# The second batch's first k^T v in place of five unread matmuls, and the first transfers in another order

## The chip, the cores and the metric

The kernel runs on one core of one Trainium2 chip. The metric is device microseconds (us) of one execution; the kernel before took 843.87 us (median of 3 runs, 843.82 to 843.91).

## The reference

Two layers are computed one after the other, all in fp32.

```python
# attention without a softmax; batch 8, heads 8, sequence 576, head size 64
kv  = np.einsum('bhsd,bhse->bhde', k, v)
out = np.einsum('bhsd,bhde->bhse', q, kv)
rms = np.sqrt(np.mean(out * out, axis=-1, keepdims=True) + 1e-06)
x   = out / rms * g_norm                     # heads side by side: x is (8, 576, 512)
# mixing along the sequence by rank 32, then a feed-forward net of 512 -> 2048 -> 512
u   = x + (x.transpose(0, 2, 1) @ U @ V).transpose(0, 2, 1)
y   = u + np.maximum(u @ w_ch1, 0.0) @ w_ch2
```

`U` is 576x32 and `V` is 32x576. The two weights `w_ch1` and `w_ch2` reach the kernel as raw bits of 64-bit numbers and are decoded on the chip.

## The kernel before, in words

**Tiling.** The eight heads of a batch are four pairs (p = 0 to 3), 128 columns each. The 8 x 576 = 4608 tokens are nine blocks of 512. The feed-forward net works block by block with 16 slices of 128 of the 2048 hidden columns: `ffn1` computes a slice of the hidden layer into a PSUM tile `h` (for slice 0 of the first block into a tile `pp`), `relu` takes it to SBUF in two fp32r parts (`hhl`, high part by ScalarE, low part by VectorE), and `ffn2` multiplies it into four accumulators `y`. A product of two fp32 numbers is three fp32r products: high by high, high by low, low by high.

**Attention of a pair.** `kv_step` multiplies k^T v (PE) and copies it into `kvb` (ScalarE); `out_step` multiplies q by it (PE) and squares it (ScalarE, L358 and L359); `stats_step` sums the squares (VectorE, L369), takes a square root (ScalarE, L370) and three or four small VectorE steps (L371 to L374); `mul_step` scales the product into `x` (VectorE, L391 and L393). `turn_step` turns `x` by a product with the identity (PE, `wf`), `t_step` and `t4_step` form x U (PE, then ScalarE and VectorE L443), `mix_first` adds the product with V (PE) and splits the result into `uth` (ScalarE, L155) and `utl` (VectorE, L485), the operands of `ffn1`; `mix_rest` does the last 64 tokens. For batch 1 and later, one `kv_step` serves two pairs: 20 matmuls from the tile `kv_sb`.

**The first stage.** Before the feed-forward net can run, pairs 0 to 3 of batch 0 go through all of this one after the other. In the same time the first weights are decoded: ScalarE makes a cast (L130, `dec_104<-raw`, one shared buffer), VectorE combines it (L133), ScalarE casts the high part (L145, `ws` or L153, `w1s`), and VectorE subtracts the low part (L146 or L165). Each engine carries out its instructions in the order in which they stand in its program.

**What sets the order.** `PLAN` gives every step of the first stage a place (a number), the steps are issued in the order of these places, and then the scheduler of the language decides, from its own estimates of durations, how the instructions of an engine follow each other. From slice 13 of block 0 on (`pinned`), matmuls keep the order in which they are written. `LOADS` is the order in which the SyncE queue issues the first 19 transfers; after the first eight of them each waits for an earlier one to land. In `LOADS`, `kv0` is k and v of pair 0, `q0` its q, `w11` the `w_ch1` half of weight slice 1, `w21` its `w_ch2` half, `uv` is U and V, and `kv4` and `q4` are the k, v and q of batch 1's first pairs. `keep_warm` issues matmuls whose results nobody reads: `fill0=3` with pair 0 and `fill1=5` with pair 1, and `FILL` another nine.

Of the kernel before, what the change touches and what calls it, by code (L numbers as in the profile page):

```python
# [58 lines left out]
PREP = [37, 37, 41, 43, 47, 49, 53, 57, 56, 63, 63, 66, 66, 69, 75, 78]  # L59
RAWAT = [-1, -1, -1, -1, -1, -1, -1, -1, -1, -1, -1, -1]  # L60
CPAT = [8, 8, 10, 12, 12, 14, 16, 18, 18, 20, 22, 24, 26, 28, 30]
PLAN = dict(g=2, pair=(2, 7.5, 10.5, 13.5), kv=(-3, 0.5, 0, -1), out=(0, 2.5, 2, 2.5), stats=(2.5, 3, 2.5, 7.0), mul=(2.5, 5.5, 4.0, 8.5), tr=(11.5, 8.5, 10.5, 12.5), t=(14.0, 11.0, 12.5, 15.0), t4=(14.5, 16, 14, 17.0), mix=(25.5, 21.5, 27, 19.5), mt=(44.0, 41.0, 38.5, 46.5), uv=-6, v4=15, w0=33, x0=53, warm=12, fill0=3, fill1=5, fill2=0, fill3=0, d=(16.5, 17.5))
ENG = dict(u0='vgg', kv='aaaaa', xh='aaaaa', xl='vvvvv', t4='aaaa', te='aaaa', uh='aaaa', v4='ggga', wh='agg', wl='vvv', ab='vvv', u='va')
LOADS = ['kv0', 'uv', 'q1', 'q0', 'w10', 'kv1', 'w11', 'kv2', 'q2', 'q3', 'kv3', 'w13', 'w22', 'w23', 'w20', 'w12', 'w21', 'kv4', 'q4']
NBLK = B * S // BLK


# [1 line left out]
def build(ctx: ExitStack, tc: tile.TileContext, kv0_in, kv_in, q_in, uv_in, w_in, out):  # L69
# [19 lines left out]
    v4 = const.tile([P, S], F32R, name="v4")  # L89
# [11 lines left out]
    def mm(*args, **kw):  # L101
        ins = nc.tensor.matmul(*args, **kw)  # L102
        if pinned[0]:
            tc.keep_in_program_order(ins)
# [16 lines left out]
    def decode(raw, tmp, n=None, held=False):  # L121

        parts = raw.bitcast(BF16).rearrange("p (n t) -> p n t", t=4)
        size = parts.shape[1]
        top = tops[:, 0:size].bitcast(FP16).rearrange("p (n t) -> p n t", t=2)[:, :, 1]
        if n is None or ENG["ab"][n] == "a":
            nc.scalar.copy(out=top, in_=parts[:, :, 2])  # L130
        else:
            nc.vector.tensor_copy(out=top, in_=parts[:, :, 2])
        ins = nc.vector.scalar_tensor_tensor(out=tmp.bitcast(U32), in0=raw.bitcast(U32).rearrange("p (n t) -> p n t", t=2)[:, :, 0],  # L133
                                             scalar=13, in1=tops[:, 0:size].bitcast(U32), op0=ALU.logical_shift_right,
                                             op1=ALU.bitwise_or)
        if held:
            tc.keep_in_program_order(ins)
# [10 lines left out]
    def move(which, n, out, in_, mul=None):  # L148

        e = ENG[which][n]  # L150
        if e == "a":
            if mul is None:
                nc.scalar.copy(out=out, in_=in_)  # L153
            else:
                nc.scalar.mul(out=out, in_=in_, mul=mul)  # L155
        else:
            eng = nc.vector if e == "v" else nc.gpsimd
            if mul is None:
                eng.tensor_copy(out=out, in_=in_)
            else:  # L160
                eng.tensor_scalar(out=out, in0=in_, scalar1=mul, scalar2=None, op0=ALU.mult)

    def minus(which, n, out, in0, in1):
        eng = nc.vector if ENG[which][n] == "v" else nc.gpsimd
        eng.tensor_tensor(out=out, in0=in0, in1=in1, op=ALU.subtract)  # L165
# [39 lines left out]
    def load_w(f, w):  # L205
        if f not in raws:
            raws[f] = weight_slot(f"raw{f}", [P, 2, DM], I64, f)
        load_fields(raws[f][:, w], w_in[f][:, w], f >= 4)

    def keep(which, f, w):  # L210
        w_sb[which][f] = [[w[:, c // 2, s, (c % 2) * P:(c % 2 + 1) * P] for c in range(ND)] for s in range(2)]

    def halves(t):
        return t.rearrange("p (a c) -> p a c", a=2)

    def decode_first(which, tmp, n):
        decode(raws.pop(which), tmp, n)
        w = const.tile([P, 2, 2, DM // 2], F32R, name=f"{which}s0", tag=f"{which}_0")
        move("wh", n, w[:, :, 0], halves(tmp))
        minus("wl", n, w[:, :, 1], halves(tmp), w[:, :, 0].bitcast(F32))  # L220
        keep(which, 0, w)
        whole[which, 0] = w

    def decode_w(f, held=False):

        tmp = dec_tile(1)
        decode(raws.pop(f).rearrange("p w c -> p (w c)"), tmp, held=held)
        w = weight_slot(f"ws{f}", [P, 4, 2, DM // 2], F32R, f)
        t = tmp.rearrange("p (a c) -> p a c", a=4)
        split(w[:, :, 0], w[:, :, 1], t, nc.vector)  # L230
        for n, which in enumerate(("w1", "w2")):
            keep(which, f, w[:, 2 * n:2 * n + 2])
        whole[f] = w
# [69 lines left out]
    def bank():  # L303
        bank_no[0] += 1
        if startup[0] and bank_no[0] % (7 - NEARLY) >= 3 - NEARLY:
            return ps_y.tile([P, 512], F32, name="y")
        return ps_p.tile([P, 512], F32, name="pp")

    def kv_step(b, p):

        if b > 0 and p % 2:
            return
        m = loads.pop(("kv", b, p))
        pp = bank()
        if b == 0:
            kb = kvb[p % 2]
            for i in range(NT):
                for lo in (0, D):
                    own = slice(i * P + lo, i * P + lo + D)
                    mm(pp[lo:lo + D, 0:D], lhsT=m[:, own], rhs=m[:, NT * P:][:, own], start=(i == 0), stop=(i == NT - 1))  # L320
            for lo in (0, D):
                move("kv", p, kb[lo:lo + D, lo:lo + D], pp[lo:lo + D, 0:D])
            return
        tails = 4 * MAIN
        for a in range(2):
            for i in range(NT):
                k, v = (2 * a * MAIN + i * P, (2 * a + 1) * MAIN + i * P) if i < 4 else (tails, tails + (1 + a) * P)
                for lo in (0, D):
                    mm(pp[lo:lo + D, a * D:(a + 1) * D], lhsT=m[:, k + lo:k + lo + D], rhs=m[:, v + lo:v + lo + D],
                       start=(i == 0), stop=(i == NT - 1))  # L330
        for lo in (0, D):
            move("kv", -1, kvbs[lo:lo + D, :, lo:lo + D], pp[lo:lo + D, 0:2 * D].rearrange("p (a c) -> p a c", a=2))
# [44 lines left out]
    def plain(b, p):  # L377
        return b < len(T32) and T32[b][p] == "f"
# [290 lines left out]
    spare = ps_h.tile([P, BLK], F32, name="h")  # L669
    for _ in range(PLAN["warm"]):  # L670
        mm(spare[:, 0:P], lhsT=kvb[0], rhs=kvb[0], start=True, stop=True)
    nc.scalar.sqrt(out=root, in_=eps)
    x123 = weight_slot("x123", [P, NPAIR - 1, NT, P], F32, 15)
    x0 = [x_sb] + [x123[:, p] for p in range(NPAIR - 1)]
# [15 lines left out]
    uv = uvs[:, NUV:NUV + NUV // 2].bitcast(F32)  # L690
# [9 lines left out]
    for w, which in enumerate(("w1", "w2")):  # L700
        first[f"{which}0"] = lambda which=which: load_first(which)
        for f in range(1, 4):
            first[f"{which}{f}"] = lambda f=f, w=w: load_w(f, w)
    for name in LOADS:
        first[name]()
# [18 lines left out]

    tasks = [(PLAN["uv"], uv_step), (PLAN["v4"], v4_step), (PLAN["g"], g_step)]
    ahead = 1 + len(PLAN["d"])
    for f, place in enumerate(PLAN["d"]):
        tasks.append((place, lambda f=f: decode_w(1 + f, True)))
    for p in range(NPAIR):
        for name, what in (("kv", kv_step), ("out", out_step), ("stats", stats_step), ("mul", mul_step),  # L730
                           ("tr", turn_step), ("t", t_step), ("t4", t4_step)):
            tasks.append((PLAN["pair"][p] + PLAN[name][p], lambda what=what, p=p: what(0, p)))
        tasks.append((PLAN["pair"][p] + PLAN["mix"][p], lambda p=p: keep_warm(p, PLAN[f"fill{p}"])))
        tasks.append((PLAN["pair"][p] + PLAN["mix"][p], lambda p=p: mix_first(p)))
        tasks.append((PLAN["pair"][p] + PLAN["mt"][p], lambda p=p: mix_rest(p)))
    for place, n in FILL:
        tasks.append((place, lambda n=n: [mm(spare[:, 0:P], lhsT=kvb[0], rhs=kvb[0], start=True, stop=True) for _ in range(n)]))
    tasks.append((PLAN["w0"], lambda: decode_first("w1", early[0], 0)))
    tasks.append((PLAN["x0"], lambda: decode_first("w2", early[1], 2)))
    def next_load(load, b, p):  # L740
        nxt = (b, p + 1) if p + 1 < NPAIR else (b + 1, 0)
        if nxt[0] < B:
            load(*nxt)

    def split_step(b, p):
        if not plain(b, p):
# [3 lines left out]
                     t=t_step, t4=t4_step)  # L750
# [8 lines left out]
    tasks = {}  # L759
# [8 lines left out]
    def pair_tasks(b, p, base, steps):  # L768


        def run(*names):
            for name in names:
                attention[name](b, p)

        def o():
            run("out", "stats", "mul", *([] if plain(b, p) else ["turn"]))

        def t():
            run("t", "t4")

        for name, what in (("kv", lambda: run("kv")), ("kvl", lambda: next_load(load_kv, b, p + 1) if p % 2 == 0 else None), ("out", o),
                           ("ql", lambda: next_load(load_q, b, p)), ("split", lambda: run("split")), ("turn", lambda: run("turn") if plain(b, p) else None), ("t", t), ("mix", lambda: mix_step(b, p))):
            at(base + steps[name], what)

# [185 lines left out]
```

## Time and profile before

| | |
|---|---|
| median of 3 runs | 843.87 us |
| profiled execution: span from the first to the last instruction | 842.3 us |
| median less span | 1.6 us |
| TensorE busy | 831.6 us (99%) |
| VectorE busy | 605.4 us (72%) |
| ScalarE busy | 380.0 us (45%) |
| first `ffn2` matmul on TensorE (row `y<-hhl,w2s`) | 41.68 us after the start |

The profiled execution is one execution; its span leaves out what lies ahead of the first and behind the last instruction, and no other time of that execution is recorded. Matmuls overlap each other, so TensorE counts as busy for nearly the whole span; where it waits is read from the bracket at the end of a row of the timeline, `[0.75 <-ACT uth L155]`: 0.75 us idle before this row, ended by the ScalarE instruction that wrote `uth`. In a timeline row the first number is the start, the second the duration of the merged run of instructions, and `xN` their count; an fp32 matmul appears as two. The start of the next row less the start of this one is what the engine was taken up for. PE is TensorE, PEld its weight loads, ACT is ScalarE, DVE VectorE, POOL GpSimd and SPq the queue of SyncE.

### The profile page before, as it was taken

The page shows a single profiled execution, that of the slowest core. Times are in us where ns is not written, and L with a number is a line of the kernel's source. Part 1 is how long each engine was busy: PE and PEld are TensorE (multiplying, and loading weights), DVE is VectorE, ACT ScalarE, POOL GpSimd, SP SyncE. Part 2 cuts the span into 40 slices and gives each one's busy share as a digit, 9 for nine tenths or more (in the row PEclk, how much of TensorE's full clock was granted, in tenths as well). Part 3 has the DMA queues.
Part 4 walks back from the last instruction along what each step waited for, and adds up shares of the span by engine and source line. Part 5 has one row for each costly group of instructions (what it writes and reads, how often), then busy time and mean ns, then how long its engine had stood idle before and what let it go on. Part 6 is the DMA issues. An engine that isn't in the chain of part 4 may idle for free.

```text
span 842.3 us, 12663 instructions
## 1 busy us (share of the span) xinstructions
PE 831.6 (99%) x4581; PEld 694.3 (82%) x4581; DVE 605.4 (72%) x991; ACT 380.0 (45%) x663; POOL 8.3 (1%) x37
## 2 busy tenths in 40 slices
PE   8999999999999999999999999999999999999998
PEld 8888888888887888888888878888888888888886
DVE  4788655778898877767957898568667965762574
ACT  4766422333244444465436653644355444332431
POOL 3000000000000000000000000000000000000000
PEclk9999999999999999999999999999999999999999
DMA  9996975666487764577878678866765786666665
GB/s 339 385 375 227 370 261 213 237 202 196 139 288 255 222 182 139 162 239 240 258 226 285 208 227 253 273 212 193 228 206 174 224 268 204 184 187 211 193 202 175
DMA packets 105229, 195.00 MB, mean 232 GB/s; under 512 B 10320, under 2 KB 41296, under 8 KB 101456
## 3 DMA queue, kind: packets, MB, share of 16 engines
q1 hardware_dynamic: 105024, 194.07, 70.4%
q8 instruction: 37, 0.61, 0.3%
q14 instruction: 24, 0.20, 0.1%
q10 hardware_dynamic: 144, 0.13, 0.0%
HBM read 142.91 MB, written 51.25 MB: 231 GB/s over the span
## 4 chain that ended last, share of the span: by engine, by line
PE 89%; DVE 5%; DMA 4%; ACT 1%; issue 1%; SPq 0%; DVEq 0%; ACTq 0%
PE y L102 67%; PE h L102 13%; PE pp L102 9%; DMA w2s<-dec 1%; DMA kvq<-kv_in 1%; DMA w2s<-wf 1%; DMA w1s<-wf 1%; DVE dec L268 1%; DVE ss L369 1%; DVE hhl L525 1%; DVE dec L273 1%; ACT wf L145 1%; DMA ringw<-w2s 1%; DVE dec L146 0%; DVE dec L133 0%
## 5 line engine op out<-in xcount | busy, mean ns | idle before, releaser
L102 PE MATMUL y<-entry,ring 128*128 128x512 f32 x576 | 136.0, 390 | 0.0
L102 PE MATMUL y<-hhl,ws 128*128 128x512 f32 x540 | 132.3, 392 | 0.0
L102 PEld LDWEIGHTS y<-entry,ring 128*128 128x128 f32 x576 | 107.5, 188 | 22.2
L102 PE MATMUL h<-uth,ws 128*128 128x512 f32 x360 | 120.4, 395 | 1.4 <-ACT uth L155 0.7
L102 PEld LDWEIGHTS y<-hhl,ws 128*128 128x128 f32 x540 | 99.9, 188 | 20.1
L594 DVE TENSOR_TENSOR h<-y,h 128x512 f32<-128x512 f32 x71 | 48.6, 689 | 57.4 <-PE y L102 52.1
L102 PE MATMUL y<-uB,ringw 128*128 128x512 f32 x354 | 85.0, 391 | 0.0
L638 DVE TENSOR_TENSOR entry<-h,entry 128x1024 fp32r<-128x1024 f32 x48 | 58.6, 1220 | 35.0 <-ACT entry L637 34.8
L102 PE MATMUL y<-uT,ring 128*128 128x512 f32 x348 | 82.4, 390 | 0.0
L102 PEld LDWEIGHTS h<-uth,ws 128*128 128x128 f32 x360 | 67.5, 188 | 16.6 <-DVE hhl L525 1.7
L102 PEld LDWEIGHTS y<-uB,ringw 128*128 128x128 f32 x354 | 66.0, 188 | 13.6
L102 PEld LDWEIGHTS y<-uT,ring 128*128 128x128 f32 x348 | 65.0, 188 | 13.6 <-ACT h L601 0.2
L637 ACT CAST entry<-h 128x1024 fp32r<-128x1024 f32 x48 | 50.5, 1052 | 44.7 <-PE y L102 44.2
L102 PE MATMUL h<-utl,ws 128*128 128x512 f32 x180 | 70.3, 391 | 0.0
L524 ACT ACTIVATE hhl<-h 128x512 fp32r<-128x512 f32 x47 | 28.0, 596 | 76.4 <-PE h L102 76.3
L102 PE MATMUL y<-hhl,ringw 128*128 128x512 f32 x216 | 55.2, 390 | 0.5 <-DMA ringw<-w2s 0.5
L102 PE MATMUL y<-entry,ringw 128*128 128x512 f32 x216 | 55.1, 390 | 0.0
L102 PE MATMUL y<-uT,ringw 128*128 128x512 f32 x210 | 51.0, 391 | 0.0
L102 PEld LDWEIGHTS y<-hhl,ringw 128*128 128x128 f32 x216 | 40.4, 188 | 9.5 <-DMA ringw<-w2s 0.9
L102 PEld LDWEIGHTS y<-entry,ringw 128*128 128x128 f32 x216 | 40.3, 188 | 8.3
L525 DVE SCALAR_TENSOR_TENSOR hhl<-h,hhl 128x512 fp32r<-128x512 f32 x47 | 32.1, 682 | 20.5 <-ACT hhl L524 20.3
L102 PEld LDWEIGHTS y<-uT,ringw 128*128 128x128 f32 x210 | 39.1, 188 | 8.2 <-issue 0.2
(200 smaller groups left out, 1185.9 us busy)
## 6 DMA issues: line engine op xcount, KB each, us to landing
ring<-wd SPq DMA_DIRECT2D x69, 256.0 KB, 3.9
kv_sb<-kv_in SPq DMA_DIRECT2D x14, 1216.0 KB, 7.8
ringw<-wd SPq DMA_DIRECT2D x66, 256.0 KB, 3.7
wd<-ws SPq DMA_DIRECT2D x15, 1024.0 KB, 8.7
raw<-w_in SPq DMA_DIRECT2D x30, 511.8 KB, 10.2
ring<-w1s SPq DMA_DIRECT2D x48, 256.0 KB, 3.6
ringw<-w1s SPq DMA_DIRECT2D x48, 256.0 KB, 3.6
ring<-w2s SPq DMA_DIRECT2D x48, 256.0 KB, 3.7
```

The lines of the kernel that those rows point to most:

```text
L102: ins = nc.tensor.matmul(*args, **kw)
L145: nc.scalar.copy(out=hi, in_=src)
L268: ins = nc.vector.tensor_tensor(out=halves(a[:, k * DM:(k + 1) * DM]), in0=w[:, :, 0].bitcast(F32), in1=w[:, :, 1].bitcast(F32), op=ALU.add)
L273: nc.vector.tensor_tensor(out=o, in0=in0, in1=in1, op=op)
L369: nc.vector.tensor_reduce(out=ss.rearrange("p (i h) -> p i h", h=2), in_=xv, axis=AX.X, op=ALU.add)
L524: nc.scalar.activation(out=hh, in_=h, func=AF.Relu)
L525: nc.vector.scalar_tensor_tensor(out=hl, in0=h, scalar=0.0, in1=hh.bitcast(F32), op0=ALU.max, op1=ALU.subtract)
L594: nc.vector.tensor_tensor(out=out, in0=in0, in1=in1, op=ALU.add)
L637: nc.scalar.copy(out=hi, in_=src)
L638: nc.vector.tensor_tensor(out=lo, in0=src, in1=hi.bitcast(F32), op=ALU.subtract)
```

## The change

Three numbers and one step are changed. `fill1` goes from 5 to 0: the five unread 128x512 matmuls with pair 1 are gone. A new task at place 26.0 calls `kv_step(1, 0)`: the 20 matmuls of the second batch's first k^T v, and the ScalarE copies behind them, are issued within the first stage, and the same step is left out of where it stood, beside slice 1 of block 0. `LOADS` now names all k, v and q of batch 0 ahead of any weight.

```diff
-PLAN = dict(..., warm=12, fill0=3, fill1=5, fill2=0, fill3=0, d=(16.5, 17.5))
+PLAN = dict(..., warm=12, fill0=3, fill1=0, fill2=0, fill3=0, d=(16.5, 17.5), next=26.0)
-LOADS = ['kv0', 'uv', 'q1', 'q0', 'w10', 'kv1', 'w11', 'kv2', 'q2', 'q3', 'kv3', 'w13', 'w22', 'w23', 'w20', 'w12', 'w21', 'kv4', 'q4']
+LOADS = ['kv0', 'uv', 'q0', 'kv1', 'q1', 'kv2', 'q2', 'kv3', 'q3', 'w11', 'w21', 'kv4', 'w12', 'w22', 'w10', 'w20', 'q4', 'w13', 'w23']
...
+    tasks.append((PLAN["next"], lambda: kv_step(1, 0)))
...
-        for name, what in (("kv", lambda: run("kv")), ...
+        for name, what in (("kv", lambda: run("kv") if (b, p) != (1, 0) else None), ...
```

Since the scheduler sets the order from its estimates, the change moves more than these lines. Outside the first stage and the first few slices of block 0 the order is the same as before. Two places matter here.

The first is VectorE between the sum of pair 3's squares (L369, the first row) and the scaling of pair 3 (L391, the last row). `dec_...<-raw_...` and `ws_...` are decodes of weight slices, `temps<-w1raw` that of slice 0, `st` a step of pairs 1 and 2. In the kernel before:

```order
L369 TENSOR_REDUCE ss<-x_123 128x10
L371 RECIPROCAL r_405<-ta 128x10
L372 TENSOR_TENSOR ta<-r_405 128x10
L373 SCALAR_TENSOR_TENSOR ta<-ss,ta 128x10
L443 TENSOR_TENSOR st<-y,st 32x128
L374 SCALAR_TENSOR_TENSOR r_405<-ta,r_405 128x10
L443 TENSOR_TENSOR st<-pp,st 32x128
L391 TENSOR_TENSOR x_123<-y,r_405 128x512
```

In the changed kernel, for the same stretch:

```order
L369 TENSOR_REDUCE ss<-x_123 128x10
L146 TENSOR_TENSOR ws_385<-dec_382,ws_385 128x4x256
L443 TENSOR_TENSOR st<-y,st 32x128
L371 RECIPROCAL r_405<-ta 128x10
L443 TENSOR_TENSOR st<-pp,st 32x128
L372 TENSOR_TENSOR ta<-r_405 128x10
L133 SCALAR_TENSOR_TENSOR dec_392<-raw_163,dec_104 128x1024
L373 SCALAR_TENSOR_TENSOR ta<-ss,ta 128x10
L132 CAST dec_104<-w1raw_166 128x512
L374 SCALAR_TENSOR_TENSOR r_405<-ta,r_405 128x10
L133 SCALAR_TENSOR_TENSOR temps<-w1raw_166,dec_104 128x512
L391 TENSOR_TENSOR x_123<-y,r_405 128x512
```

Four decode instructions (`ws_385`, `dec_392`, `dec_104<-w1raw`, `temps<-w1raw`) now stand ahead of pair 3's scaling; a fifth (`dec_382`) stands two places ahead of the first row shown. All five stood behind it before.

The second is ScalarE around pair 3's result (`uth<-pp`, the operand of the last quarter of `ffn1`) and the first relu (`hhl<-pp`). In the kernel before:

```order
L145 CAST ws_395<-dec_392 128x4x256
L155 ACTIVATE uth<-pp,g_sb 128x512
L155 ACTIVATE ut_3_94<-pp,g_sb 128x64
L153 CAST w1s_470<-temps 128x2x256
L145 CAST uth<-ut_3_94 128x64
L153 COPY kvb<-pp 64x2x64 x2
L130 CAST dec_104<-raw_162 128x1024
L524 ACTIVATE hhl<-pp 128x512
```

In the changed kernel:

```order
L130 CAST dec_104<-raw_172 128x1024
L145 CAST ws_549<-dec_546 128x4x256
L130 CAST dec_104<-raw_175 128x1024
L155 ACTIVATE uth<-pp,g_sb 128x512
L155 ACTIVATE ut_3_94<-pp,g_sb 128x64
L145 CAST uth<-ut_3_94 128x64
L145 CAST ws_585<-dec_582 128x4x256
L130 CAST dec_104<-raw_178 128x1024
L358 ACTIVATE xh<-pp 128x512
L524 ACTIVATE hhl<-pp 128x512
```

The decodes of slice 3 (`raw_172`, `ws_549`) and the first half of slice 4's (`raw_175`) moved ahead of pair 3's result; the rest of slice 4's, the first of slice 5's and a square of batch 1 (`xh`) moved ahead of the first relu. Before, one cast of slice 3 (`raw_162`) stood between the two.

## Rows read from the trace of the kernel before

**Rows 1.** Spans by core, with the mean granted clock of TensorE.
```profile
core 0: 842.3 us, clock 1.000
```

**Rows 2.** Timeline of TensorE, 0 to 42 us (start, us, engine, line).
```profile
1.06 5.49 PE L102 MATMUL h<-kvb 128*128 128x128 f32 x24 [1.06 <-DVE eps L668]
...
9.06 2.17 PE L102 MATMUL h<-kvb 128*128 128x128 f32 x18
...
17.66 1.16 PE L102 MATMUL pp<-wf,x 128*128 128x128 f32 x8 [0.28 <-DVE x L391]
...
21.41 1.28 PE L102 MATMUL y<-kvb,kvq 128*128 128x128 f32 x10
...
25.72 1.44 PE L102 MATMUL h<-v,st 128*128 128x512 f32 x5
26.99 0.40 PE L102 MATMUL pp<-v,st 128*128 128x256 f32 x2
...
27.46 1.05 PE L102 MATMUL pp<-wf,x 128*128 128x128 f32 x8
...
35.12 0.51 PE L102 MATMUL h<-uth,ws 128*128 128x512 f32 x1 [0.75 <-ACT uth L155]
...
36.49 1.39 PE L102 MATMUL pp<-kv_sb 128*64 128x64 f32 x40
...
41.68 0.71 PE L102 MATMUL y<-hhl,w2s 128*128 128x512 f32 x2
```

**Rows 3.** Timeline of VectorE, 15 to 42 us.
```profile
20.87 0.27 DVE L393 TENSOR_TENSOR x<-y,r 64x128 f32<-64x128 f32 x1
...
23.35 0.82 DVE L369 TENSOR_REDUCE ss<-x 128x10 f32<-128x640 f32 x1 [0.27 <-ACT x L359]
...
26.85 0.27 DVE L393 TENSOR_TENSOR x<-y,r 64x128 f32<-64x128 f32 x1
27.25 1.23 DVE L133 SCALAR_TENSOR_TENSOR dec<-raw,dec 128x1024 uint32<-128x1024 uint32 x1
28.40 0.74 DVE L485 SCALAR_TENSOR_TENSOR utl<-pp,g_sb,uth 128x512 fp32r<-128x512 f32 x1
...
29.72 1.21 DVE L146 TENSOR_TENSOR ws<-dec,ws 128x1024 fp32r<-128x1024 f32 x1
...
33.36 0.47 DVE L132 CAST dec<-w1raw 128x512 f16<-128x512 bf16 x1
33.86 0.69 DVE L133 SCALAR_TENSOR_TENSOR temps<-w1raw,dec 128x512 uint32<-128x512 uint32 x1
```

**Rows 4.** Timeline of ScalarE, 15 to 46 us.
```profile
25.85 1.38 ACT L130 CAST dec<-raw 128x1024 f16<-128x1024 bf16 x1
...
28.59 1.04 ACT L145 CAST ws<-dec 128x1024 fp32r<-128x1024 f32 x1
...
34.38 0.69 ACT L155 ACTIVATE uth<-pp,g_sb 128x512 fp32r<-128x512 f32 x1 [0.25 <-PE pp L102]
...
40.85 0.60 ACT L524 ACTIVATE hhl<-pp 128x512 fp32r<-128x512 f32 x1 [1.00 <-PE pp L102]
...
43.99 0.61 ACT L358 ACTIVATE xh<-pp 128x512 f32<-128x512 f32 x1
```

**Rows 5.** Transfers issued in 0 to 30 us: count, KB each, median us to landing.
```profile
raw<-w_in SPq DMA_DIRECT2D x14, 511.8 KB, 11.2
kvq<-kv_in SPq DMA_DIRECT2D x4, 640.5 KB, 9.1
...
kvq<-q_in SPq DMA_DIRECT2D x4, 288.0 KB, 7.8
...
uvs<-uv_in SPq DMA_DIRECT2D x1, 303.8 KB, 4.4
```

**Rows 6.** Busy time by stretch; the last columns are granted clock, DMA share, GB/s.
```profile
0.00:10.00 10.00, 8.40 (x63) 8.04 (x64) 1.52 (x7) 4.93 (x13) 5.85 (x30) 1.00 0.80 266
10.00:20.00 10.00, 8.92 (x114) 7.98 (x113) 6.62 (x20) 4.09 (x15) 1.67 (x6) 1.00 1.02 403
```

More of the change, by code (lines that the diff above doesn't have):

```diff
@@ L61 @@
 CPAT = [8, 8, 10, 12, 12, 14, 16, 18, 18, 20, 22, 24, 26, 28, 30]
-PLAN = dict(g=2, pair=(2, 7.5, 10.5, 13.5), kv=(-3, 0.5, 0, -1), out=(0, 2.5, 2, 2.5), stats=(2.5, 3, 2.5, 7.0), mul=(2.5, 5.5, 4.0, 8.5), tr=(11.5, 8.5, 10.5, 12.5), t=(14.0, 11.0, 12.5, 15.0), t4=(14.5, 16, 14, 17.0), mix=(25.5, 21.5, 27, 19.5), mt=(44.0, 41.0, 38.5, 46.5), uv=-6, v4=15, w0=33, x0=53, warm=12, fill0=3, fill1=5, fill2=0, fill3=0, d=(16.5, 17.5))
+PLAN = dict(g=2, pair=(2, 7.5, 10.5, 13.5), kv=(-3, 0.5, 0, -1), out=(0, 2.5, 2, 2.5), stats=(2.5, 3, 2.5, 7.0), mul=(2.5, 5.5, 4.0, 8.5), tr=(11.5, 8.5, 10.5, 12.5), t=(14.0, 11.0, 12.5, 15.0), t4=(14.5, 16, 14, 17.0), mix=(25.5, 21.5, 27, 19.5), mt=(44.0, 41.0, 38.5, 46.5), uv=-6, v4=15, w0=33, x0=53, warm=12, fill0=3, fill1=0, fill2=0, fill3=0, d=(16.5, 17.5), next=26.0)
 ENG = dict(u0='vgg', kv='aaaaa', xh='aaaaa', xl='vvvvv', t4='aaaa', te='aaaa', uh='aaaa', v4='ggga', wh='agg', wl='vvv', ab='vvv', u='va')
-LOADS = ['kv0', 'uv', 'q1', 'q0', 'w10', 'kv1', 'w11', 'kv2', 'q2', 'q3', 'kv3', 'w13', 'w22', 'w23', 'w20', 'w12', 'w21', 'kv4', 'q4']
+LOADS = ['kv0', 'uv', 'q0', 'kv1', 'q1', 'kv2', 'q2', 'kv3', 'q3', 'w11', 'w21', 'kv4', 'w12', 'w22', 'w10', 'w20', 'q4', 'w13', 'w23']
 NBLK = B * S // BLK
@@ L779, in t @@
             run("t", "t4")
-        for name, what in (("kv", lambda: run("kv")), ("kvl", lambda: next_load(load_kv, b, p + 1) if p % 2 == 0 else None), ("out", o),
+        for name, what in (("kv", lambda: run("kv") if (b, p) != (1, 0) else None), ("kvl", lambda: next_load(load_kv, b, p + 1) if p % 2 == 0 else None), ("out", o),
                            ("ql", lambda: next_load(load_q, b, p)), ("split", lambda: run("split")), ("turn", lambda: run("turn") if plain(b, p) else None), ("t", t), ("mix", lambda: mix_step(b, p))):
```

## The prediction

> **What bounds the kernel now.** First the span: 842.3 us on the one core [rows 1], 1.6 us under the median of 843.87. Then the timeline of TensorE over the first 42 us, the only stretch that the change touches [rows 2]. The reader is to see two things there. Up to the row `y<-hhl,w2s` at 41.68 the attention of batch 0 and the first slices of the net are being prepared; from there the net runs, and the new order of the instructions differs little. And in this stretch TensorE hardly waits: 0.28 us at 17.66, 0.75 us at 35.12, the rest is smaller. What carries the time over is the start of that row: each us by which 41.68 moves moves the end, because behind it TensorE is the bound. Then the timelines of VectorE and ScalarE for the same stretch [rows 3, 4], because four pairs hand their work from PE to ScalarE to VectorE and back, and it is there that the new order places the weight decodes.
>
> **Part 1: what goes and what moves on TensorE.** The five unread matmuls run from 25.72 to 26.99: 1.27 us [rows 2]. The 20 matmuls of `kv_sb` take 1.39 us at 36.49, in a stretch without slack; they move to about the place of the five. Pair 3's k^T v moves ahead of the turn of pair 1 and fills the wait in front of 17.66; with the smaller ones around it I count 0.9 us, so that pair 3's product with q starts at 20.5 instead of 21.41. By TensorE alone, from that product to the first `ffn2` matmul there were 41.68 - 21.41 = 20.3 us: 1.3 of unread matmuls, some 1.9 of waits and gaps (0.75 of them at 35.12), 17.1 of work. Without any wait the row would come at 20.5 + 17.1 = 37.6; the relu behind the last `ffn1` needs about 0.9 us on top (0.60 us for its first half, row at 40.85 [rows 4], and the handing over), part of it beside five matmuls of batch 1, and the waits at pair 3's result remain in part: 39.5, or 2.2 us less. This is the end of the range for a change that does nothing but this.
>
> **Part 2: the decodes in front of pair 3.** VectorE ended pair 2's scaling at 20.87 + 0.27 = 21.14 and pair 3's at 26.85 + 0.27 = 27.12 [rows 3]. In the new order five decode instructions come in between. Their prices: `dec_382` and `dec_392` 1.15 us each (27.25 to 28.40), `ws_385` 1.2 (row at 29.72), the cast of slice 0 0.47, `temps` 0.69: 4.7 us. Pair 3's own part, from its sum of squares to the end of its scaling, took 27.12 - 23.35 = 3.8 us, 0.6 of them waits that the decodes now fill, but `dec_392` waits for its ScalarE cast (1.38 us, [rows 4]), which stands behind casts of pairs 1 and 2; I put that at 0.4. One `utl` is 0.7. Sum: 4.7 + 3.2 + 0.4 + 0.7 = 9.0, less some 0.1 where instructions overlap. It starts 0.4 later than before, at 21.5, since on ScalarE pair 2's square root now stands behind a 1.38 us cast of `raw_158`. So pair 3 is scaled at 30.4, 3.3 us later than before. Between 8.4 (no wait at all) and 9.6 I take 8.9.
>
> TensorE came to the turn of pair 3 at 27.46 without a wait [rows 2]. Now it comes there at 27.46 - 1.27 + 0.7 (three matmuls of `ffn1` moved ahead) + 1.4 (`kv_sb`) - 0.7 = 27.6, and waits until 30.25, when the larger part of the scaling is done: 2.65 us, twice what the five matmuls took.
>
> **Part 3: the decodes in front of pair 3's result and of the relu.** From 30.4 VectorE has `ws_395` 1.2, a cast 0.45, two `utl` 1.4 and 0.7 + 0.7 for slice 0: it ends these at 34.8. `dec_104` is one buffer, so ScalarE's cast of slice 3 cannot start before the last of them; it also stands behind small casts that come from TensorE's last turns, which end at 35.1. Then one waits for the other: ScalarE 1.38 (36.5), VectorE 1.2 (37.75), ScalarE 1.0 (38.75), ScalarE 1.35 for slice 4 (40.1), and only then `uth` of pair 3, 0.65: 40.75. Before it was done at 34.38 + 0.69 = 35.07 [rows 4]. TensorE has its input for it at 38.0 and has nothing else: 2.8 us idle. Behind `uth` ScalarE has 0.6 of small steps, the high part of slice 4 (to 42.3), the cast of slice 5 (1.36: 43.65), a square of batch 1 (0.6 by the row at 43.99, with overlap 44.2) and then the first relu: 44.8. First `ffn2` matmul: 44.85 against 41.68, so **+3.15 us**. Check by TensorE: 20.5 + 17.1 of work + idle 0.35 (`ws_385` late) + 2.65 + 2.8 + 1.65 = 45.0.
>
> **Part 4: the transfers.** k, v, q, U and V of batch 0 are 4 x (640.5 + 288.0) + 303.8 KB = 4.1 MB [rows 5]; at 266 GB/s for 10 us and 403 behind it [rows 6] they land by 13.6 us and the two halves of slice 1 by 16.2. ScalarE asks for slice 1 at 17.5. Counted by the 11.2 us to landing of a `raw` [rows 5] from an issue at 6.5 it would be 17.7. So the weights cost nothing to 0.5 us; I take nothing. k and v of pairs 1 and 2 come earlier than needed; what pair 1 gains is 0.1 us, because nine unread matmuls keep TensorE until 11.23 (9.06 + 2.17). Behind 45 us the same instructions remain, with two slices decoded ahead; a gain or loss of 0.3 us either way is possible there, none is taken.
>
> Sum: 842.3 + 3.15 = 845.4 for the span, **847.0 us** beside the median.
>
> **The rivals.** *TensorE alone decides.* If VectorE had pair 3 scaled by the time TensorE is there, the gain of part 1 would be left: 843.87 - 2.2 = 841.7. The point from which it decides is 27.6 us. For it: in the kernel before TensorE hardly waits, though decodes run beside it. Against it: VectorE would need to do 8.4 us of instructions in 6.1.
>
> *The two cancel.* The wait at pair 3 comes, but the later decodes are done when `uth` is due, since VectorE and ScalarE run somewhat faster than my starts say; then the row comes at 30.25 + 10.4 of work = 40.7 plus up to 1.2 us behind the relu: 40.9 to 42.0, so 843.1 to 844.2. For it: 2 us out of 19 us of handing over decide. Against it: the waits of part 3 are in one row, each for the one before, and their prices are single instructions with rows.
>
> *The clock falls in the new idle time.* The first 24 halves of unread matmuls took 5.49 us, 0.229 each, the later 18 took 2.17, 0.121 each [rows 2]: the two levels, 1.2 and 2.4 GHz, though the granted clock in the rows reads 1.00 throughout. In the kernel before nothing tests a pause of 2.65 us, or of 2.8. If the matmuls behind the first pause ran at the lower level for as long as at the start, 5.2 us, up to 2.6 us would be added, and pair 3's result is late by it: 849.5. The Trainium skill, "TensorE: Matmul & The Clock Gate" (section "Part 1: The HAM clock gate"), says that the throttled clock is the default and that it comes back after the array was idle; this case's start agrees, 0.229 against 0.121 us. By that rule the removed matmuls were the cover, and their going speaks against this change.
>
> **How the numbers follow.** Differences up to 0.2%, 1.7 us, cannot be told from no change. Chances: forecast 0.62 (847.0, its own range 845.2 to 848.6), the clock 0.10 (849.5), the two cancel 0.15 (843.7), TensorE alone 0.13 (841.7). Slower by over 0.2% (above 845.6) holds the clock and nearly all of the forecast: 0.71. Within it: 0.16. Faster (below 842.2): 0.13. The range leaves out TensorE alone and what lies above the clock's price: 843.0 to 849.5.
>
> **What would show it.** In the new trace the row of pair 3's turn (`pp<-wf,x`, after `kv_sb`) starts at 30.2 with a bracket of 2 to 3 us that names `DVE x L391`; `uth` of pair 3 ends near 40.7 and not near 35; a wait of 2 to 3 us in front of `pp<-uth,w1s` names ScalarE; `y<-hhl,w2s` starts near 44.9. If that row starts before 41 the forecast is wrong, and part 2 or 3 with it: part 2 if the bracket at pair 3's turn is under 1 us, part 3 if the bracket is there and `uth` still ends by 38. If FFN matmuls behind a pause take twice their 0.23 us, it is the clock.

## The result, and the profile after

The changed kernel took 849.78 us (median of 11 runs, 845.24 to 854.65) beside 843.91 us for the kernel before on the same chip: ratio of the runs 1.006, 95% interval 1.0042 to 1.0078 (the two medians alone give 1.007). It is slower, as forecast; the time lies 2.8 us above the forecast of 847.0 and 0.3 us above the end of the range. The profiled execution took 847.73 us, less than most of its runs. Its span answers to [rows 1]:

```profile
core 0: 845.6 us, clock 0.998
```

First the timeline of TensorE, which answers to [rows 2].

```profile
20.53 1.28 PE L102 MATMUL y<-kvb,kvq 128*128 128x128 f32 x10
...
25.52 1.39 PE L102 MATMUL y<-kv_sb 128*64 128x64 f32 x40
...
29.81 1.62 PE L102 MATMUL pp<-wf,x 128*128 128x128 f32 x8 [2.24 <-DVE x L391]
31.22 1.92 PE L102 MATMUL y<-x,wf 128*96 128x128 f32 x8
...
41.52 0.50 PE L102 MATMUL pp<-uth,w1s 128*128 128x512 f32 x1 [1.71 <-ACT uth L155]
...
45.68 3.00 PE L102 MATMUL y<-hhl,w2s 128*128 128x512 f32 x12 [1.17 <-ACT hhl L524]
```

Three new waits stand in the brackets: 2.24 us for pair 3's scaling, 1.71 us for pair 3's result, 1.17 us for the relu. Then one more thing is to be seen: the eight matmuls at 29.81 took 1.62 us, where the same eight took 1.05 us in the kernel before, and the eight behind them 1.92 us. The stretches of TensorE (length, busy time and count, granted clock, DMA share, GB/s) say why:

```profile
25.00:30.00 5.00, 2.76 (x48) 1.00 1.03 408
30.00:35.00 5.00, 5.00 (x26) 0.66 1.02 406
35.00:40.00 5.00, 4.80 (x23) 1.00 1.01 412
40.00:45.00 5.00, 3.00 (x16) 1.00 0.90 308
```

In the 5 us behind the first wait the granted clock is 0.66: TensorE was at the lower of its two levels (1.2 and 2.4 GHz) for much of them. VectorE, which answers to [rows 3], from pair 2's scaling to pair 3's:

```profile
21.06 0.27 DVE L393 TENSOR_TENSOR x<-y,r 64x128 f32<-64x128 f32 x1
21.26 1.21 DVE L133 SCALAR_TENSOR_TENSOR dec<-raw,dec 128x1024 uint32<-128x1024 uint32 x1
...
23.78 1.21 DVE L146 TENSOR_TENSOR ws<-dec,ws 128x1024 fp32r<-128x1024 f32 x1
...
26.59 1.23 DVE L133 SCALAR_TENSOR_TENSOR dec<-raw,dec 128x1024 uint32<-128x1024 uint32 x1 [0.51 <-ACT dec L130]
...
28.34 0.69 DVE L133 SCALAR_TENSOR_TENSOR temps<-w1raw,dec 128x512 uint32<-128x512 uint32 x1
29.07 0.69 DVE L391 TENSOR_TENSOR x<-y,r 128x512 f32<-128x512 f32 x1
29.67 0.27 DVE L393 TENSOR_TENSOR x<-y,r 64x128 f32<-64x128 f32 x1
```

The decodes stand between the two scalings, and pair 3's ends at 29.94 instead of 27.12. ScalarE, which answers to [rows 4], from slice 3's cast to the relu:

```profile
34.04 0.31 ACT L155 ACTIVATE ut<-y,g_sb 128x64 f32<-128x64 f32 x1 [2.91 <-PE y L102]
...
35.99 1.35 ACT L130 CAST dec<-raw 128x1024 f16<-128x1024 bf16 x1
38.63 1.05 ACT L145 CAST ws<-dec 128x1024 fp32r<-128x1024 f32 x1 [1.29 <-DVE dec L133]
39.59 1.33 ACT L130 CAST dec<-raw 128x1024 f16<-128x1024 bf16 x1
40.80 0.67 ACT L155 ACTIVATE uth<-pp,g_sb 128x512 fp32r<-128x512 f32 x1
...
44.95 0.58 ACT L524 ACTIVATE hhl<-pp 128x512 fp32r<-128x512 f32 x1
```

The two casts (35.99 and 39.59) stand in front of pair 3's `uth`, which ends at 41.47 instead of 35.07. And ScalarE itself waited 2.91 us for TensorE's last turns, which ran at the lower clock (in a later profile in which the clock stays at 1.00, the same wait is 1.34 us): so the clock pushes this whole chain. Of the transfers, [rows 5], k and v of a pair land sooner (6.6 us against 9.1) and the first raw weights of slice 0 later (13.5 against 6.9; count, KB each, median us to landing):

```profile
kvq<-kv_in SPq DMA_DIRECT2D x4, 640.5 KB, 6.6
...
w1raw<-w_in SPq DMA_DIRECT2D x1, 511.8 KB, 13.5
```

### The profile page after: what moved, and what is told of

It is laid out like the page before. It is cut to its first block, busy times and chain, and to the rows that moved or that the text cites. A ratio compares the mean times of both kernels' runs of the same rounds, so it can differ in the third digit from the quotient of the medians.

```text
span 845.6 us, 12662 instructions
## 1 busy us (share of the span) xinstructions
PE 831.8 (98%) x4576; PEld 694.7 (82%) x4576; DVE 604.8 (72%) x991; ACT 380.4 (45%) x663; POOL 8.3 (1%) x37
## 4 chain that ended last, share of the span: by engine, by line
PE 82%; DMA 7%; DVE 7%; ACT 2%; issue 1%; DVEq 0%; SPq 0%; ACTq 0%
PE y L102 64%; PE h L102 11%; PE pp L102 7%; DMA raw<-w_in 4%; DVE dec L268 1%; DMA w2s<-dec 1%; DVE dec L273 1%; DMA w2s<-wf 1%; DVE dec L146 1%; DVE hhl L525 1%; DMA w1s<-wf 1%; ACT wf L145 1%; DMA w1s<-dec 1%; DVE dec L133 1%; DMA kvq<-q_in 1%
## 5 line engine op out<-in xcount | busy, mean ns | idle before, releaser
L102 PEld LDWEIGHTS y<-uT,ring 128*128 128x128 f32 x348 | 65.0, 188 | 13.5
```

## The experiments

A theory of two parts was tested. The order: decodes in front of pair 3's scaling and of its result hold TensorE up. The clock: without the unread matmuls TensorE stands idle, and then runs slower. "Before" has its own median in each group of runs (843.2 to 844.1 us; for the last two profiles a single run, 842.88), and the ratios are to it. What is read from a trace is read from one execution.

**The parts by themselves.** The new order of transfers alone, in the kernel before:

```diff
-LOADS = ['kv0', 'uv', 'q1', 'q0', 'w10', ...]
+LOADS = ['kv0', 'uv', 'q0', 'kv1', 'q1', ...]
```

> Only the new order of the transfers; the five unread matmuls stay and the k^T v of batch 1 stays in slice 1. Theory (early weights let the scheduler put five decodes in front of pair 3's scaling): pair 3 is scaled near 29.5 instead of 27.1, TensorE waits about 2 us for it, the first ffn2 matmul starts near 44 and the median is 845.5 to 847.5, above that if the clock falls in the wait. Rival (the k^T v taken out of its place and the missing five matmuls cost the time; the transfers are harmless): no decode in front of pair 3 matters, first ffn2 matmul by 41.7, median 843.9 or less.

It took 848.97 us, ratio 1.0055 (1.0038 to 1.0072). TensorE:

```profile
29.68 1.16 PE L102 MATMUL pp<-wf,x 128*128 128x128 f32 x8 [1.52 <-DVE x L391]
...
44.38 3.31 PE L102 MATMUL y<-hhl,w2s 128*128 128x512 f32 x12 [1.47 <-ACT hhl L524]
```

The wait at pair 3's turn is there though the five unread matmuls run before it, and the clock stays at 1.00. On VectorE the same five decode instructions stand in front of pair 3's scaling (21.11 to 28.90) as in the change. So the order of the transfers is what brings them to the front, and it costs more than was expected. Of the 4.9 us, 2.7 are there at the first `ffn2` (44.38 against 41.68); the rest lies behind it and is not explained.

The early k^T v at place 26 without the unread matmuls, transfers as before:

```diff
-LOADS = ['kv0', 'uv', 'q0', 'kv1', 'q1', ...]   # in the changed kernel
+LOADS = ['kv0', 'uv', 'q1', 'q0', 'w10', ...]
```

> Only the early k^T v in place of the five unread matmuls; the transfers in the order of before. Theory: pair 3 is scaled at 27.1 as before, TensorE waits under 1 us for it; in the order of this kernel pair 3's last step still stands behind the decodes of slices 0 to 2 and its result behind two casts, so the second wait stays: first ffn2 matmul 42.5 to 44.5, median 844.5 to 847. Rival (the moved k^T v is the cause of all of it): the wait in front of pair 3's turn is 2 us or more and the median is as with the whole change, 848 or more.

It took 852.13 us, ratio 1.0089 (1.0066 to 1.0113). TensorE, and two stretches of it:

```profile
27.10 1.52 PE L102 MATMUL pp<-wf,x 128*128 128x128 f32 x10 [0.22 <-DVE x L391]
...
43.27 0.79 PE L102 MATMUL pp<-uth,w1s 128*128 128x512 f32 x1 [3.98 <-ACT uth L155]
```

```profile
40.00:45.00 5.00, 1.73 (x6) 0.76 0.61 182
45.00:50.00 5.00, 5.00 (x18) 0.55 1.02 377
```

The first wait is gone as expected, the second is larger than ours, 3.98 us, and behind it the granted clock falls to 0.55. The size was missed by 5 us.

The early k^T v alone, at place 29, where the other engines keep nearly the order of the kernel before, with the unread matmuls and the old transfers:

```diff
-PLAN = dict(..., fill1=0, ..., next=26.0)       # in the changed kernel, LOADS as before
+PLAN = dict(..., fill1=5, ..., next=29)
```

> The kernel before with one part of the change: the second batch's first k^T v is taken out of its old place and issued at place 29 of the plan; the five unread matmuls and the old order of transfers stay. In the new order no decode stands in front of pair 3's scaling on VectorE, as in the kernel before. Theory (what costs is the decodes that the new order of transfers lets in front of pair 3, and TensorE idle): the move by itself is harmless: the wait at pair 3's turn stays under 0.5 us, the first ffn2 starts at 41.0 to 42.5 us, 843 to 845 us. Rival (the early k^T v itself does harm, by its ScalarE and VectorE steps): 846 us or more.

It took 844.11 us, ratio 1.0005 (0.9996 to 1.0014): the move is harmless, as expected, and gains nothing. Its first `ffn2` matmul starts at 40.72, 1 us earlier than in the kernel before, but the last matmul ends at 838.60 against 838.73: in this execution TensorE waits three times behind that row, 0.29 to 0.39 us, up to 60 us, and 0.96 us for a transfer at 535.

The same without the unread matmuls (`fill1=0`):

> As the run before in this call, without the five unread matmuls, the old order of transfers still. Slice 0's decode then falls behind pair 3 on VectorE. Theory with the clock: no wait of over 0.6 us at pair 3's turn, but a wait of 1.5 to 3 us behind the relu since the decodes held back come there, the granted clock under 0.9 in 40 to 50 us, the first ffn2 at 42.5 to 44.5 us: 846 to 850 us. Theory without the clock: 844 to 846.5 us. Rival (1.27 us of unread matmuls less is 1.27 us gained): 841.5 to 843 us.

It took 849.62 us, ratio 1.0074 (1.0059 to 1.0089). None of the three cases fits whole: the time is that of the first, but the clock stays at 1.00 from 20 us on. It had fallen before that:

```profile
8.37 2.35 PE L102 MATMUL y<-kvb,kvq 128*128 128x128 f32 x10 [1.72 <-DMA kvq<-q_in]
...
14.73 1.13 PE L102 MATMUL y<-kvb,kvq 128*128 128x128 f32 x8 [0.64 <-issue]
```

```profile
5.00:10.00 5.00, 3.28 (x36) 0.85 0.97 319
10.00:15.00 5.00, 4.36 (x44) 0.81 1.03 405
```

The row at 14.73 stands at 12.82 in the run before, so 1.9 of the 6.0 us by which the first `ffn2` is later (46.74 against 40.72) come from a wait for pair 0's q and from the clock behind it, both well ahead of the place of the five. The other 4.1 come from new waits (0.70 us at 32.92, 1.68 us for slice 0's weights, 2.12 us for the relu), in an order in which slice 0's decode stands behind pair 3's `utl`. So this run does not price the waits cleanly; all six of its executions have a mean clock of 0.997 or 0.998, but only this one has a profile.

The kernel before without its unread matmuls:

```diff
-PLAN = dict(..., fill1=5, ...)
+PLAN = dict(..., fill1=0, ...)
```

> The kernel before without the five unread matmuls, nothing else of the change. Slice 0's decode falls behind pair 3 on VectorE. Theory: nothing is late at pair 3's turn (wait under 0.6 us), but the decodes held back come in front of the relu, TensorE waits there 1 to 3 us: the first ffn2 at 42 to 44 us, 844 to 848 us, nearer the upper end if the granted clock falls under 0.9 in 40 to 50 us. Rival (unread matmuls only cost TensorE time): 842.0 to 843.2 us.

It took 853.41 us, ratio 1.0114 (1.01 to 1.0128), slower than the change itself. TensorE:

```profile
38.62 0.79 PE L102 MATMUL pp<-uth,w1s 128*128 128x512 f32 x1 [2.26 <-ACT w1s L153]
48.36 0.87 PE L102 MATMUL y<-hhl,w2s 128*128 128x512 f32 x2 [3.56 <-ACT hhl L524]
```

The direction is the theory's, the size again too small. Taking out 1.27 us of unread work put slice 0's decode behind pair 3's `utl` (`temps<-w1raw` starts at 37.23, before at 33.86); as nothing else was edited, the scheduler must count these matmuls in its estimates. TensorE waited 2.26 and 3.56 us, and the granted clock was 0.79 to 0.87 in the stretches from 35 to 55 us.

**Decodes held back.** In the change, slices 1 and 2 are decoded at later places:

```diff
-PLAN = dict(..., d=(16.5, 17.5), next=26.0)
+PLAN = dict(..., d=(26, 30), next=26.0)
```

> The whole change, but the decodes of slices 1 and 2 have the places 26 and 30 in place of 16.5 and 17.5, so that they stand behind pair 3's scaling on VectorE and pair 3's result stands in front of the cast of slice 3 on ScalarE. Theory: pair 3 is scaled by 28, TensorE waits under 1 us for it, uth of pair 3 ends by 36, the first ffn2 matmul starts at 40 to 41 and the median is 841.5 to 843. Rival (the moved k^T v or the missing matmuls are the cause): first ffn2 matmul at 44 or later and 847 or more. Rival (the clock alone): it falls here too, as nothing covers TensorE, and the runs scatter over several us.

It took 849.91 us, ratio 1.0071 (1.0052 to 1.009), so the expected time was missed by 7 us. TensorE, and one stretch:

```profile
27.39 1.16 PE L102 MATMUL pp<-wf,x 128*128 128x128 f32 x8 [0.47 <-DVE x L391]
...
43.67 4.70 PE L102 MATMUL y<-hhl,w2s 128*128 128x512 f32 x12 [2.58 <-ACT hhl L524]
```

```profile
45.00:50.00 5.00, 5.00 (x17) 0.75 1.01 370
```

Pair 3 is early as expected, and with the new transfers still in place the wait in front of its turn is down to 0.47 us: it was the decodes that made it. But slice 0's decode is late in its place: ScalarE's cast of slice 3 waits 1.84 us for it, to 38.12, and the wait of TensorE moves to the relu. The twelve `ffn2` matmuls behind it took 4.70 us where the change needed 3.00: the clock again. This execution is the slowest of the six (852.63 us), and part of its time is lost much later, behind a wait for a transfer:

```profile
508.10 1.49 PE L102 MATMUL y<-hhl,ringw 128*128 128x512 f32 x3 [2.29 <-DMA ringw<-w2s]
```

Behind this wait, too, the granted clock falls: 0.83 in 505 to 515 us. In the kernel before the wait at this place is 0.48 us and the clock stays at 1.00.

**The unread matmuls put back.** The change with five of them, and with eight:

```diff
-PLAN = dict(..., fill1=0, ...)
+PLAN = dict(..., fill1=5, ...)                   # fill1=8 in the next
```

> The whole change with the five unread matmuls back, now in a stretch where TensorE waits for pair 3. Theory with the clock: they cost nothing in time, the wait in front of pair 3's turn shrinks from 2.2 to about 1 us, the granted clock stays at 1.00 there, the first ffn2 matmul starts near 44.3 (1.3 earlier than with the whole change), and the median is 845.5 to 847 with less scatter. Without the clock (the waits alone): first ffn2 matmul as with the whole change or up to 1.3 later, same scatter, median 849.5 to 851.

> The change with eight unread matmuls. VectorE, ScalarE, GpSimd and the transfer queue have the very order that they have in the change with five; only TensorE differs, by three more of the matmuls. With nine, ScalarE also had pair 3's result in front of the cast of slice 4, so two things differed there. If the unread matmuls alone were the gain of the nine (846.1 us with five, 843.7 with nine): the wait at pair 3's turn under 0.4 us and 843.8 to 845.2 us. If the place of that cast was the gain: the wait for pair 3's result stays at 1.5 to 2 us, granted clock under 0.8 in 40 to 45 us, 845.6 to 847 us.

With five it took 846.13 us, ratio 1.0025 (1.0013 to 1.0037), 12 runs from 845.12 to 848.43; with eight 846.52 us, 1.0035 (1.0023 to 1.0047), 845.34 to 847.40. With five, the waits at pair 3's turn and for its result are 0.57 and 1.84 us. The granted clock stays at 1.00 at the turn, as expected, but is 0.66 in 40 to 45 us, behind the second wait:

```profile
40.00:45.00 5.00, 5.00 (x20) 0.66 0.99 371
```

And that fall costs nothing here: the first `ffn2` starts at 44.16 (expected near 44.3), without a wait in front of it, and with eight, where the clock stays at 1.00, at 44.23 behind a wait of 1.18 us. The slower matmuls only fill the time in which TensorE would have waited for the relu.

The decodes in front of pair 3's scaling are the same in these two and in the change (ahead of its result, only slice 0's `w1s` and some small steps change places), and yet the change takes 3.3 to 3.7 us longer (2.5 to 3.8 when each is taken from the kernel before beside it) and scatters over 9.4 us where these scatter over 3.3 and 2.1. TensorE and ScalarE with eight:

```profile
29.86 1.16 PE L102 MATMUL pp<-wf,x 128*128 128x128 f32 x8 [0.57 <-DVE x L391]
40.07 0.49 PE L102 MATMUL pp<-uth,w1s 128*128 128x512 f32 x1 [1.17 <-ACT uth L155]
44.23 3.00 PE L102 MATMUL y<-hhl,w2s 128*128 128x512 f32 x12 [1.18 <-ACT hhl L524]
```

```profile
34.53 1.35 ACT L130 CAST dec<-raw 128x1024 f16<-128x1024 bf16 x1
...
39.34 0.68 ACT L155 ACTIVATE uth<-pp,g_sb 128x512 fp32r<-128x512 f32 x1
```

Pair 3's turn starts at the same time as in the change (29.86 against 29.81), but its eight matmuls take 1.16 us, slice 3's cast starts 1.46 us earlier (34.53 against 35.99) and the first `ffn2` 1.45 us earlier. The turn waits 0.57 us here instead of 2.24; the time is the same, it is only filled. Three more than five bring nothing, so the unread matmuls alone did not make the gain of the next run. Of the case that was expected for this, only the time fits: the wait for pair 3's result is 1.17 us and not 1.5 to 2, and the clock in 40 to 45 us is 1.00 and not under 0.8.

The change with nine:

> The change with nine unread matmuls at the place where the kernel before had five. They fill the whole wait that the change has at pair 3's turn (2.24 us at 0.25 us each), and in this order pair 3's result on ScalarE comes in front of the cast of slice 4. Theory with the clock: granted clock 1.00 in 25 to 40 us, wait at pair 3's turn 0 to 0.3 us, wait for its result 0 to 1 us, the first ffn2 at 42.5 to 44 us: 844 to 846 us, faster than the change by 4 to 5 us. Rival (unread matmuls only cost TensorE time): the first ffn2 at 46 us or later, 849 us or more.

It took 843.68 us, ratio 0.9997 (0.9986 to 1.0009), as fast as the kernel before and a little less than expected. With nine the scheduler also puts pair 3's result ahead of slice 4's cast on ScalarE. ScalarE, then TensorE, then a stretch of it:

```profile
37.67 0.69 ACT L155 ACTIVATE uth<-pp,g_sb 128x512 fp32r<-128x512 f32 x1 [0.70 <-PE pp L102]
...
38.45 1.36 ACT L130 CAST dec<-raw 128x1024 f16<-128x1024 bf16 x1
```

```profile
29.46 1.16 PE L102 MATMUL pp<-wf,x 128*128 128x128 f32 x8 [0.35 <-DVE x L391]
...
42.80 3.00 PE L102 MATMUL y<-hhl,w2s 128*128 128x512 f32 x12
```

```profile
35.00:40.00 5.00, 5.00 (x17) 0.67 1.03 421
```

ScalarE now waits for TensorE (0.70 us, with TensorE at the lower clock) and not the other way round, and no wait is left in front of `ffn2`. Between eight and nine lie 2.8 us of the median. Of these 1.43 are there at the first `ffn2` (44.23 and 42.80) and come with this order of ScalarE's casts (the relu, too, has one of them less in front of it); the rest lies behind it. In these two executions a wait for a transfer, 1.27 us at 504 against 0.63 at 502, makes some of it. The expected clock of 1.00 to 40 us did not hold: it was 0.67 in 35 to 40.

The kernel before with eight, all else in its old order:

> The kernel before with eight unread matmuls instead of five; every other instruction stands in its old order on every engine. TensorE waits for nothing at that place in the kernel before, so three more take 0.76 us of its time there, of which the 0.75 us wait behind them at 35.12 may hide up to all. Theory (unread matmuls are worth something only where TensorE would stand idle): 843.8 to 844.7 us, not faster. Rival (any unread matmul makes the kernel faster): under 843.2 us.

It took 844.82 us beside 843.17, ratio 1.0016 (1.0002 to 1.0029). Unread matmuls are no gain where nothing waits: the first `ffn2` is 1.04 us later, 42.72 (0.35 of it is there at 13.12 already, ahead of them). The time itself, 1.65 us up, is more than their 0.76 us; the interval is too wide to say more.

**The change once more.** Two further profiles of the changed kernel:

> The change itself, once more with a profile, to see where its slower runs lose their time: its runs lie between 845.2 and 854.7 us, those with a mean granted clock of 1.0 near 846.6, those with 0.994 near 853. Theory with the clock: beside 0.66 in 30 to 35 us, stretches below 0.9 stand behind the later waits (40 to 50 us) in a run of 849 us or more, and the first waits have the lengths of the first profile (2.2 and 1.7 us). Rival (later transfers or waits scatter): the first ffn2 starts within 0.5 us of 45.7 and the time is lost behind 346 us.

> As the run before in this call: a third profile of the change. Of the time that lies between the profiles of the change, the theory puts most into the first 60 us and at granted clocks below 1.0; the rival puts it behind 346 us.

They took 845.00 and 847.32 us beside 842.88, both with a mean clock of 1.000, so neither was one of the slower runs, and where those lose their time stays unseen. But they show the change without the fall of the clock. Of the first of them, TensorE, a stretch of it, and ScalarE:

```profile
29.66 1.16 PE L102 MATMUL pp<-wf,x 128*128 128x128 f32 x8 [2.23 <-DVE x L391]
...
39.80 0.50 PE L102 MATMUL pp<-uth,w1s 128*128 128x512 f32 x1 [1.72 <-ACT uth L155]
...
43.97 2.99 PE L102 MATMUL y<-hhl,w2s 128*128 128x512 f32 x12 [1.19 <-ACT hhl L524]
```

```profile
30.00:35.00 5.00, 5.00 (x33) 1.00 1.02 405
```

```profile
34.27 1.36 ACT L130 CAST dec<-raw 128x1024 f16<-128x1024 bf16 x1
...
39.06 0.68 ACT L155 ACTIVATE uth<-pp,g_sb 128x512 fp32r<-128x512 f32 x1
```

The three waits are those of the first profile to 0.02 us. In one execution the clock fell behind the first of them and in two it did not: first `ffn2` at 45.68, 43.97 and 43.82. With the clock kept, the first `ffn2` starts no earlier with eight unread matmuls (44.23) than with none. Of the two cases that were expected neither fits: no clock fell in the first 60 us, and the 2.3 us between the two new ones do not lie behind 346 us but between 196 and 278, where one of them has a wait of 1.59 us at 198 us.

## Why the prediction was right, and by what it was off

**Part 1** held: pair 3's product with q starts at 20.53 (predicted 20.5), and k^T v takes 1.39 us at its new place.

**Part 2** held: the five decode instructions stand there, the scaling ends at 29.94 (predicted 30.4), and the bracket of 2.24 us (predicted 2.65) names VectorE. That the transfers cause it was not in the prediction and is shown by the first run: it has the wait, and the kernels with the old transfers have none over 0.5 us at this turn. That it is the decodes is shown by the run that holds them back: new transfers, and 0.47 us.

**Part 3** held in its mechanism: from the start of slice 3's cast to the end of `uth` were predicted 40.75 - 35.1 = 5.65 us, and 5.48 us were measured in the first profile and 39.74 - 34.27 = 5.47 us in the second. The run with nine unread matmuls, whose order takes slice 4's cast out of this chain, shows that the order of the casts decides: 1.43 us at the first `ffn2` between eight and nine.

**The sum** was too large for the waits: with the clock kept, the first `ffn2` comes at 43.97 and 43.82, 2.2 us behind [rows 2] and not 3.15. Some 0.6 to 0.7 us of the difference are there at pair 3's turn already (29.66 and 29.51, predicted 30.25). The three waits were put at 2.65 + 2.8 + 1.65 = 7.1 us and are 2.23 + 1.72 + 1.19 = 5.1; that the check by TensorE (45.0) is only 1.0 us off is luck, as what lies between them took some 18.5 us and not 17.1 + 0.35. Outside the span the forecast added 1.6 us, and every run of the change has 2.0 to 2.2 there.

**Part 4 and what follows.** Slice 1's cast did not wait for its transfer (17.51, no bracket), so nothing was lost there, as taken. That behind 41.68 only 0.3 us either way were possible was wrong: from the first `ffn2` to the last matmul the kernel before took 797.05 us, the three profiles of the change 796.05, 795.04 and 797.50. Waits in this part differ between executions of one kernel: the three have 1.02, no and 0.31 us at about 274, none, 0.25 and 0.15 us for a transfer at about 503, and the third alone has the 1.59 us at 198.

**What failed is the chance of the clock.** The prediction gave it 0.10 and counted it at nothing. The first profile has it behind the first pause; there it costs 45.68 less 43.97 or 43.82, 1.7 to 1.9 us, against 2.6 us priced (from 5.2 us at the lower level, where the row of the start gives 5.49). The step that failed is this: two pauses of two us each, which the kernel before does not have, were taken to leave the clock as it was.

How much of the median this made is an estimate. Over the runs the mean granted clock goes with the time: the four at 1.000 (845.00, 846.39, 846.79, 847.32) average 846.4 us, 0.6 us below the forecast, and the six at 0.997 or less lie at 849.78 to 854.65. The median run, 849.78 us, has 0.996 over a span of 847.7 us, which is 847.7 x 0.004 = 3.4 us of full clock less, and 846.4 + 3.4 = 849.8. So the waits are worth some 2.5 us of the 5.9 and the clock up to 3.4. This is not shown: two runs do not fit (845.24 us at 0.998, 849.12 us at 0.999), a longer wait can cost time and bring the clock down with it, as at 508 us in the run with the decodes held back, and a lower clock need not cost time. With five unread matmuls, seven runs at 0.997 or 0.998 average 845.9 us and five at 0.999 or 1.000 average 847.0. Nor is the kernel before free of it: of 62 of its runs beside the experiments, six at 0.996 or 0.997 average 845.8 us and 51 at 0.999 or 1.000 average 843.4.

The experiments also split the loss by the parts of the change. By medians, each less the kernel before beside it, the new transfers alone cost 4.9 us; with the early k^T v added, 2.1; and with the five unread matmuls then taken out, which is the change, 5.9. So the early k^T v gains 2.8 us once the transfers are new, though it gained nothing with the old ones (at place 29), and the missing unread matmuls cost 3.8. The prediction's sum has them only as 1.27 us less of work.

The Trainium skill, "TensorE: Matmul & The Clock Gate" (section "Part 1: The HAM clock gate"), says of the start of a kernel that how many matmuls run at the lower clock differs from run to run of the same kernel. The three profiles show the like behind a pause: 0.66, 1.00 and 1.00 behind the same wait. With such a difference between executions a single price for the rival, and a single profile after, could not have been enough.

What stays open: in runs of 850 us and more the clock must fall further than in the first profile (a mean of 0.994 to 0.997 against 0.998), but none was profiled, so whether behind the second and third wait, as in the runs with 0.55 and 0.75 there, or behind a wait for a transfer, as at 508 us, is not shown. No version beat the kernel before.

## What to carry to other kernels

An unread matmul has three effects that have to be priced apart: its own time, the idle time that it fills, in which the clock could fall, and its weight in a scheduler's estimates, which here moved other engines' work by more than it costs itself. The order of transfers decides through that same scheduler which work stands in front of which, so look first at what a new order puts ahead of the instruction that the bounding engine waits for. Where new pauses of some us appear on TensorE, give the fall of its clock a chance near that of the waits, and profile more than one execution. A fall is to be priced by its place: in front of a wait it can cost nothing.

## What the runs showed of the hardware that was not expected

The same wait of 2.23 to 2.25 us was followed by a granted clock of 0.66 in one execution and of 1.00 in two. Nor need a long wait stand just in front of a fall: in the change with nine unread matmuls TensorE waited 0.45 and 0.35 us and was busy in all of 30 to 40 us, and still had 0.67 in the second half of it. And a fall can cost nothing: with five unread matmuls the clock was 0.66 in 40 to 45 us, and the first `ffn2` started at 44.16, with eight and 1.00 at 44.23.
